# Linear attention and ELU MLP in one kernel: state update fused on VectorE, one kd on ScalarE, an earlier second product, and a split first slice

## The chip, the cores and the metric

The kernel runs on one core of one Trainium2 chip. The metric is the device time of one execution in microseconds (us); lower is better. Six executions fell into a slower state: granted TensorE clocks of 0.856 to 0.992 (0.998 to 1.0 in the fast ones), times of 216.61 to 238.4 us. They are named where they occur, and only fast runs are compared. The profile covers a span some 2 us shorter than the device time of its run: 213.9 us of 215.73 for the kernel before.

## The reference

Two operations follow each other. A decaying linear attention runs over 4 batches, 8 heads, 768 positions and 64 elements per head; its output, as 3072 rows of 512, goes through a two-layer MLP with ELU and 2048 hidden columns.

```python
for b in range(nb):                                   # blocks of positions
    intra = (qb @ kb.T * Dmask) @ vb                  # einsums shortened here
    inter = (qb * lam_pow) @ kv_state
    out[block] = intra + inter
    kv_state = lam_block * kv_state + (kb * rev_pow).T @ vb
h = x @ w_in
g = where(h > 0, h, exp(min(h, 0)) - 1)
return g @ w_out
```

The line that the change is about is the one that updates `kv_state`: an old state times a decay of its head, plus an update.

## The kernel before

The kernel works in chunks `g` of 128 rows of one batch, 24 in all, gathered into tiles of 4, 2, 4, 4, 4, 4 and 2 chunks. One tile passes through 16 slices of 128 hidden columns: the first product `psH`, `e = exp(psH)` and `r = relu(psH)` on ScalarE, `g = min(e - 1, r)` on VectorE, the second product `psM`. The attention of later tiles is put between these. The state of a pair of chunks is updated in two instructions, decay on GpSimd and add on VectorE:

```python
def att_tmp(g, eng="p"):                    # GpSimd: tmp = old state * decay
    ...
    for hh in range(2):
        r = slice(hh * 64, (hh + 1) * 64)
        e.tensor_tensor(
            out=tmp[r], in0=old[r, :, :, r],
            in1=up_p[r].unsqueeze(1).unsqueeze(3).broadcast_to([64, 2, HP, 64]),
            op=ALU.mult,
        )
def att_st(g):                              # VectorE: new state = tmp + psU
    ...
                nc.vector.tensor_tensor(
                    out=new[r, :, :, r], in0=tmps[g][r], in1=pu[r], op=ALU.add
                )
```

From chunk 8 on, q and k are transposed by DMAs that SyncE issues, one for q and one for k of a pair of chunks:

```python
def att_xT(g):
    for j, ts in enumerate((qn, kn)):
        ...
        nc.sync.dma_start_transpose(
            out=dst[:], in_=heads(ts, g, 2).rearrange("p h d -> p (h d)")
        )
```

The loads of later q, k and v are issued by GpSimd. Each is held back by a copy of one element of some g, so that it is not issued before the MLP has come to that point.

```python
def paced_load(s, items):
    ...
        src = gt[t][0:1, n - w, 0:1] if n else gt[t - 1][0:1, NF - 1, 0:1]
        nc.gpsimd.tensor_copy(pace[:], src)
    run_loads(items)

for s, a, b in [(('B', 2), 27, 28), ((1, 2), 28, 29), ((1, 10), 29, 30), ...]:
    at(s, paced_load, s, LOADS[a:b])
```

`(1, 10)` is slice 10 of the second tile, and the element is one of g of the slices just before it, 8 and 9. The load that it paces is that of chunks 12 and 13.

Of the kernel before, what the change touches and what calls it, by code (L numbers as in the profile page):

```python
# [11 lines left out]
ALU = mybir.AluOpType  # L12
# [3 lines left out]
def kernel(  # L16
# [10 lines left out]
    nc = tc.nc  # L27
# [56 lines left out]
    WO = [4, 4, 4, 4]  # L84
# [28 lines left out]
    LOADS = [(0, 1, 'q'), (0, 1, 'k'), (1, 1, 'q'), (1, 1, 'k'), (2, 1, 'q'), (2, 1, 'k'), (3, 1, 'q'), (3, 1, 'k'), (0, 1, 'v'), (1, 1, 'v'), (2, 1, 'v'), (3, 1, 'v'), ('wi', 0), ('wi', 1), ('wi', 2), ('wi', 3), ('kd', 0), ('wi', 4), ('wi', 5), ('kd', 2), ('wi', 6), ('wo', 0), ('wo', 1), (4, 2), ('wo', 2), ('wo', 3), (6, 2), (8, 2), (10, 2), (12, 2), (14, 2), (16, 2), (18, 2), (20, 2), (22, 2)]  # L113

    def run_loads(items):
        for it in items:
            if it[0] == "wi":
                emit_wi(it[1])
            elif it[0] == "wo":
                emit_wo(it[1])  # L120
            elif it[0] == "kd":
                att_kd(it[1], 2, "p")
            else:
                emit_load(*it)

    nc.gpsimd.iota(rel_i[:], pattern=[[1, 128]], base=0, channel_multiplier=-1)
    run_loads(LOADS[:16])

# [173 lines left out]
    def att_S(g, tag="S"):  # L302
        s = ps.tile([128, 2, HP, 128], FP32, tag=tag, bufs=2, name=f"psS{g}")
        for hp in range(HP):
            for hh in range(2):
                r = slice(hh * 64, (hh + 1) * 64)
                nc.tensor.matmul(  # L307
                    s[:, hh, hp, :], lhsT=kT[g][r, hp, :], rhs=qT[g][r, hp, :],
                    start=True, stop=True,
                )  # L310
        pS[g] = s

    def att_mask(g, parts=1):
        P = asb.tile([128, 2, HP, 128], FP16, tag="P", name=f"P{g}", bufs=3)
        s = pS.pop(g)
        w = HP // parts
        for i in range(parts):
            c = slice(i * w, (i + 1) * w)
            nc.vector.tensor_tensor(  # L319
                out=P[:, :, c], in0=s[:, :, c],  # L320
                in1=(mask if g < B else mask1)[:, :, c], op=ALU.mult,
            )
        Pt[g] = P

    def att_O(g, n, tag="S"):
        c = g // B
        po = ps.tile([128, n, HP, 128], FP32, tag=tag, bufs=2, name=f"psO{g}")
        for i in range(n):
            P = Pt.pop(g + i)
            for hp in range(HP):  # L330
                for hh in range(2):
                    r = slice(hh * 64, (hh + 1) * 64)
                    nc.tensor.matmul(  # L333
                        po[r, i, hp, :], lhsT=v_of(g + i, 2 * hp + hh), rhs=P[:, hh, hp, :],
                        start=True, stop=(c == 0), skip_group_check=True,
                    )
                if c == 0:
                    continue
                for hh in range(2):
                    r = slice(hh * 64, (hh + 1) * 64)  # L340
                    nc.tensor.matmul(  # L341
                        po[r, i, hp, :],
                        lhsT=st[(g + i) % B // 2][c % 2][:, (g + i) % 2, hp, r],
                        rhs=qT[g + i][:, hp, :],
                        start=False, stop=True, skip_group_check=True,
                    )
        pS["O", g] = po

    def att_X(g, n, parts=1):
        t, i = where[g]  # L350
        if i == 0:
            xt[t] = asb.tile([128, HP, TS[t] * L], FP16, tag="xt", name=f"xt{t}")
        po = pS.pop(("O", g))
        w = HP // parts
        for j in range(parts):
            c = slice(j * w, (j + 1) * w)
            dst = xt[t][:, c, i * L : (i + n) * L].rearrange("p h (n l) -> p n h l", n=n)
            if g < B:
                copy = nc.vector.tensor_copy if g in () else nc.scalar.copy
                copy(out=dst, in_=po[:, :, c])  # L360
                continue
            nc.vector.tensor_tensor(  # L362
                out=dst, in0=po[:, :, c],
                in1=qs[:, c].unsqueeze(1).broadcast_to([128, n, w, 128]),
                op=ALU.mult,
            )
# [20 lines left out]
    def att_tmp(g, eng="p"):  # L387
        c, b = divmod(g, B)
        if c >= NC - 1 or c == 0:
            return  # L390
        old = st[b // 2][c % 2]
        tmp = asb.tile([128, 2, HP, 64], FP32, tag="tmp", name=f"tmp{g}", bufs=3)
        e = nc.vector if eng == "v" else nc.gpsimd
# [7 lines that stand above are left out]
        tmps[g] = tmp  # L401

    def att_st(g):
        c, b = divmod(g, B)
        if c == NC - 1:
            return
        pu = pS.pop(("U", g))
        new = st[b // 2][(c + 1) % 2]
        for hh in range(2):
            r = slice(hh * 64, (hh + 1) * 64)  # L410
            if c == 0:
                copy = nc.scalar.copy if g in () else nc.vector.tensor_copy
                copy(out=new[r, :, :, r], in_=pu[r])
            else:
                nc.vector.tensor_tensor(  # L415
                    out=new[r, :, :, r], in0=tmps[g][r], in1=pu[r], op=ALU.add
                )
        tmps.pop(g, None)
# [113 lines left out]
    def warm(k, tag="M"):  # L532
        if k <= 0:
            return
        pw = ps.tile([128, 4, 128], FP32, tag=tag, bufs=2, name=f"psW{len(warms)}")
        warms.append(pw)
        for _ in range(k):
            nc.tensor.matmul(
                pw[:, 0:2], lhsT=ident16[:], rhs=any16[:, 0:2], start=True, stop=True
            )  # L540
# [20 lines left out]
    W = [10, 4, 3, 1, 2, 1, 2, 1, 3, 2, 2, 3]  # L561
# [34 lines left out]
    warm(W[8])  # L596
    att_O(0, 1, "M")
    att_X(0, 1)
    att_S(3)
    att_mask(3, 2)  # L600
    late_qs(1, 2)
    warm(W[9])
    att_O(1, 1, "M")
    att_X(1, 1)
    late_qs(2, 3)
    warm(W[10])
    att_O(2, 1, "M")
    att_X(2, 1)
    late_qs(3, 4)
    warm(W[11])  # L610
    att_OX2(3, "H")

    run_loads(LOADS[16:27])
# [8 lines left out]
    XT = {8: ('B', 13), 10: (1, 12), 12: (2, 4), 14: (2, 12), 16: (3, 4), 18: (3, 12), 20: (4, 4), 22: (4, 12)}  # L622

    def visit(g, s0, s1, s2):
        if g in XT:
            at(XT[g], att_xT, g)
        else:
            at(s0, att_T, g, 2, "q")
            at(s0, att_T, g, 2, "k")
            at(s0, att_Te, g, 2, "q", "a")  # L630
            at(s0, att_Te, g, 2, "k", "v" if g in () else "a")
        if g not in ():
            at(s0, att_kd, g, 2, "p" if g in () else "a" if g in () else "v")
        at(s1, att_S, g)
        at(s1, att_S, g + 1)
        at(s1, att_mask, g)
        at(s1, att_mask, g + 1)
        if g in ():
            at(s1, att_kd, g, 2, "p" if g in () else "a" if g in () else "v")
        at(s2, att_O, g, 2)  # L640
        at(s2, att_U, g)
        at(s2, att_X, g, 2)
        at(s2, att_st, g)
        at(s2, att_tmp, g + B)

    for g, vs in [(4, (('B', 1), ('B', 4), ('B', 7))), (6, (('B', 12), (1, 0), (1, 4))), (8, ((1, 6), (1, 10), (1, 14))), (10, ((2, 0), (2, 2), (2, 5))), (12, ((2, 8), (2, 10), (2, 13))), (14, ((3, 0), (3, 2), (3, 5))), (16, ((3, 8), (3, 10), (3, 13))), (18, ((4, 0), (4, 2), (4, 5))), (20, ((4, 8), (4, 10), (4, 13))), (22, ((5, 0), (5, 2), (5, 5)))]:
        visit(g, *vs)
# [9 lines left out]
    for s, a, b in [(('B', 2), 27, 28), ((1, 2), 28, 29), ((1, 10), 29, 30), ((2, 3), 30, 31), ((2, 11), 31, 32), ((3, 3), 32, 33), ((3, 11), 33, 34), ((4, 3), 34, 35)]:  # L657
        at(s, paced_load, s, LOADS[a:b])

    steps = [(('A', 0), (0, 0), []), (('A', 1), (0, 1), []), (('A', 2), (0, 2), []), (('A', 3), (0, 3), []), (('A', 4), (0, 4), []), (('A', 5), (0, 5), []), (('A', 6), (0, 6), []), (('A', 7), (0, 7), []), (('A', 8), (0, 8), []), (('A', 9), (0, 9), []), (('A', 10), (0, 10), []), (('A', 11), (0, 11), []), (('A', 12), (0, 12), [(0, 0, 0), (0, 1, 0)]), (('A', 13), (0, 13), [(0, 0, 1), (0, 1, 1)]), (('A', 14), (0, 14), [(0, 0, 2), (0, 1, 2)]), (('A', 15), (0, 15), [(0, 0, 3), (0, 1, 3)]), (('B', 0), None, [(0, 2, 0), (0, 2, 1), (0, 2, 2), (0, 2, 3)]), (('B', 1), None, [(0, 3, 0), (0, 3, 1), (0, 3, 2), (0, 3, 3)]), (('B', 2), None, [(0, 0, 4), (0, 1, 4), (0, 2, 4), (0, 3, 4)]), (('B', 3), None, [(0, 0, 5), (0, 1, 5), (0, 2, 5), (0, 3, 5)]), (('B', 4), None, [(0, 0, 6), (0, 1, 6), (0, 2, 6), (0, 3, 6)]), (('B', 5), None, [(0, 0, 7), (0, 1, 7), (0, 2, 7), (0, 3, 7)]), (('B', 6), None, [(0, 0, 8), (0, 1, 8), (0, 2, 8), (0, 3, 8)]), (('B', 7), None, [(0, 0, 9), (0, 1, 9), (0, 2, 9), (0, 3, 9)]), (('B', 8), None, [(0, 0, 10), (0, 1, 10), (0, 2, 10), (0, 3, 10)]), (('B', 9), None, [(0, 0, 11), (0, 1, 11), (0, 2, 11), (0, 3, 11)]), (('B', 10), None, [(0, 0, 12), (0, 1, 12), (0, 0, 13), (0, 1, 13)]), (('B', 11), None, [(0, 0, 14), (0, 1, 14), (0, 0, 15), (0, 1, 15)]), (('B', 12), None, [(0, 2, 12), (0, 3, 12), (0, 2, 13), (0, 3, 13)]), (('B', 13), None, [(0, 2, 14), (0, 3, 14), (0, 2, 15), (0, 3, 15)]), ((1, 0), (1, 0), []), ((1, 2), (1, 2), []), ((1, 4), (1, 4), []), ((1, 6), (1, 6), [(1, 0, 0), (1, 1, 0), (1, 0, 1), (1, 1, 1)]), ((1, 8), (1, 8), [(1, 0, 2), (1, 1, 2), (1, 0, 3), (1, 1, 3)]), ((1, 10), (1, 10), [(1, 0, 4), (1, 1, 4), (1, 0, 5), (1, 1, 5)]), ((1, 12), (1, 12), [(1, 0, 6), (1, 1, 6), (1, 0, 7), (1, 1, 7)]), ((1, 14), (1, 14), [(1, 0, 8), (1, 1, 8), (1, 0, 9), (1, 1, 9)]), ((2, 0), (2, 0), [(1, 0, 10), (1, 0, 11)]), ((2, 1), (2, 1), [(1, 0, 12), (1, 0, 13)]), ((2, 2), (2, 2), [(1, 0, 14), (1, 0, 15), (1, 1, 10)]), ((2, 3), (2, 3), [(1, 1, 11), (1, 1, 12)]), ((2, 4), (2, 4), [(1, 1, 13), (1, 1, 14)]), ((2, 5), (2, 5), [(1, 1, 15), (2, 0, 0), (2, 0, 1)]), ((2, 6), (2, 6), [(2, 0, 2), (2, 0, 3)]), ((2, 7), (2, 7), [(2, 0, 4)]), ((2, 8), (2, 8), [(2, 0, 5), (2, 1, 0)]), ((2, 9), (2, 9), [(2, 0, 6), (2, 1, 1)]), ((2, 10), (2, 10), [(2, 0, 7), (2, 1, 2)]), ((2, 11), (2, 11), [(2, 0, 8), (2, 1, 3)]), ((2, 12), (2, 12), [(2, 0, 9), (2, 1, 4)]), ((2, 13), (2, 13), [(2, 0, 10), (2, 1, 5)]), ((2, 14), (2, 14), [(2, 0, 11), (2, 1, 6)]), ((2, 15), (2, 15), [(2, 0, 12), (2, 1, 7)]), ((3, 0), (3, 0), [(2, 0, 13), (2, 1, 8), (2, 0, 14), (2, 1, 9)]), ((3, 1), (3, 1), [(2, 0, 15), (2, 1, 10), (2, 1, 11), (2, 1, 12)]), ((3, 2), (3, 2), [(2, 1, 13), (2, 1, 14), (2, 1, 15), (2, 2, 0)]), ((3, 3), (3, 3), [(2, 2, 1), (2, 2, 2), (2, 2, 3), (2, 2, 4), (2, 2, 5)]), ((3, 4), (3, 4), [(2, 2, 6), (2, 2, 7), (2, 2, 8), (2, 2, 9)]), ((3, 5), (3, 5), [(2, 2, 10), (2, 2, 11), (2, 2, 12), (2, 2, 13)]), ((3, 6), (3, 6), [(2, 2, 14), (2, 2, 15), (2, 3, 0), (2, 3, 1), (2, 3, 2)]), ((3, 7), (3, 7), [(2, 3, 3), (2, 3, 4), (2, 3, 5), (2, 3, 6)]), ((3, 8), (3, 8), [(2, 3, 7), (2, 3, 8), (2, 3, 9), (2, 3, 10)]), ((3, 9), (3, 9), [(2, 3, 11), (2, 3, 12), (2, 3, 13), (2, 3, 14), (2, 3, 15)]), ((3, 10), (3, 10), [(3, 0, 0), (3, 0, 1), (3, 0, 2), (3, 0, 3)]), ((3, 11), (3, 11), [(3, 0, 4), (3, 0, 5), (3, 1, 0), (3, 0, 6)]), ((3, 12), (3, 12), [(3, 1, 1), (3, 0, 7), (3, 1, 2), (3, 0, 8), (3, 1, 3)]), ((3, 13), (3, 13), [(3, 0, 9), (3, 1, 4), (3, 0, 10), (3, 1, 5)]), ((3, 14), (3, 14), [(3, 0, 11), (3, 1, 6)]), ((3, 15), (3, 15), [(3, 0, 12), (3, 1, 7)]), ((4, 0), (4, 0), [(3, 0, 13), (3, 1, 8), (3, 0, 14), (3, 1, 9)]), ((4, 1), (4, 1), [(3, 0, 15), (3, 1, 10), (3, 1, 11), (3, 1, 12)]), ((4, 2), (4, 2), [(3, 1, 13), (3, 1, 14), (3, 1, 15), (3, 2, 0)]), ((4, 3), (4, 3), [(3, 2, 1), (3, 2, 2), (3, 2, 3), (3, 2, 4), (3, 2, 5)]), ((4, 4), (4, 4), [(3, 2, 6), (3, 2, 7), (3, 2, 8), (3, 2, 9)]), ((4, 5), (4, 5), [(3, 2, 10), (3, 2, 11), (3, 2, 12), (3, 2, 13)]), ((4, 6), (4, 6), [(3, 2, 14), (3, 2, 15), (3, 3, 0), (3, 3, 1), (3, 3, 2)]), ((4, 7), (4, 7), [(3, 3, 3), (3, 3, 4), (3, 3, 5), (3, 3, 6)]), ((4, 8), (4, 8), [(3, 3, 7), (3, 3, 8), (3, 3, 9), (3, 3, 10)]), ((4, 9), (4, 9), [(3, 3, 11), (3, 3, 12), (3, 3, 13), (3, 3, 14), (3, 3, 15)]), ((4, 10), (4, 10), [(4, 0, 0), (4, 0, 1), (4, 0, 2), (4, 0, 3)]), ((4, 11), (4, 11), [(4, 0, 4), (4, 0, 5), (4, 1, 0), (4, 0, 6)]), ((4, 12), (4, 12), [(4, 1, 1), (4, 0, 7), (4, 1, 2), (4, 0, 8), (4, 1, 3)]), ((4, 13), (4, 13), [(4, 0, 9), (4, 1, 4), (4, 0, 10), (4, 1, 5)]), ((4, 14), (4, 14), [(4, 0, 11), (4, 1, 6)]), ((4, 15), (4, 15), [(4, 0, 12), (4, 1, 7)]), ((5, 0), (5, 0), [(4, 0, 13), (4, 1, 8), (4, 0, 14), (4, 1, 9)]), ((5, 1), (5, 1), [(4, 0, 15), (4, 1, 10), (4, 1, 11), (4, 1, 12)]), ((5, 2), (5, 2), [(4, 1, 13), (4, 1, 14), (4, 1, 15), (4, 2, 0)]), ((5, 3), (5, 3), [(4, 2, 1), (4, 2, 2), (4, 2, 3), (4, 2, 4), (4, 2, 5)]), ((5, 4), (5, 4), [(4, 2, 6), (4, 2, 7), (4, 2, 8), (4, 2, 9)]), ((5, 5), (5, 5), [(4, 2, 10), (4, 2, 11), (4, 2, 12), (4, 2, 13)]), ((5, 6), (5, 6), [(4, 2, 14), (4, 2, 15), (4, 3, 0), (4, 3, 1), (4, 3, 2)]), ((5, 7), (5, 7), [(4, 3, 3), (4, 3, 4), (4, 3, 5), (4, 3, 6)]), ((5, 8), (5, 8), [(4, 3, 7), (4, 3, 8), (4, 3, 9), (4, 3, 10)]), ((5, 9), (5, 9), [(4, 3, 11), (4, 3, 12), (4, 3, 13), (4, 3, 14), (4, 3, 15)]), ((5, 10), (5, 10), [(5, 0, 0), (5, 0, 1), (5, 0, 2), (5, 0, 3)]), ((5, 11), (5, 11), [(5, 0, 4), (5, 0, 5), (5, 1, 0), (5, 0, 6)]), ((5, 12), (5, 12), [(5, 1, 1), (5, 0, 7), (5, 1, 2), (5, 0, 8), (5, 1, 3)]), ((5, 13), (5, 13), [(5, 0, 9), (5, 1, 4), (5, 0, 10), (5, 1, 5)]), ((5, 14), (5, 14), [(5, 0, 11), (5, 1, 6)]), ((5, 15), (5, 15), [(5, 0, 12), (5, 1, 7)]), ((6, 0), (6, 0), [(5, 0, 13), (5, 1, 8), (5, 0, 14), (5, 1, 9), (5, 0, 15)]), ((6, 2), (6, 2), [(5, 1, 10), (5, 1, 11), (5, 1, 12), (5, 1, 13), (5, 1, 14)]), ((6, 4), (6, 4), [(5, 1, 15), (5, 2, 0), (5, 2, 1), (5, 2, 2), (5, 2, 3), (5, 2, 4)]), ((6, 6), (6, 6), [(5, 2, 5), (5, 2, 6), (5, 2, 7), (5, 2, 8), (5, 2, 9)]), ((6, 8), (6, 8), [(5, 2, 10), (5, 2, 11), (5, 2, 12), (5, 2, 13), (5, 2, 14)]), ((6, 10), (6, 10), [(5, 2, 15), (5, 3, 0), (5, 3, 1), (5, 3, 2), (5, 3, 3), (5, 3, 4)]), ((6, 12), (6, 12), [(5, 3, 5), (5, 3, 6), (5, 3, 7), (5, 3, 8), (5, 3, 9)]), ((6, 14), (6, 14), [(5, 3, 10), (5, 3, 11), (5, 3, 12), (5, 3, 13), (5, 3, 14), (5, 3, 15)]), (('E', 0), None, [(6, 0, 0), (6, 0, 1), (6, 0, 2), (6, 0, 3), (6, 0, 4), (6, 0, 5), (6, 0, 6), (6, 0, 7), (6, 0, 8), (6, 0, 9), (6, 0, 10), (6, 0, 11), (6, 0, 12), (6, 0, 13), (6, 0, 14), (6, 0, 15), (6, 1, 0), (6, 1, 1), (6, 1, 2), (6, 1, 3), (6, 1, 4), (6, 1, 5), (6, 1, 6), (6, 1, 7), (6, 1, 8), (6, 1, 9), (6, 1, 10), (6, 1, 11), (6, 1, 12), (6, 1, 13), (6, 1, 14), (6, 1, 15)])]  # L660
    for s, m1, m2 in steps:
        er = None
        if m1 is not None:
            t, n = m1
            er = mm1(t, n, alt=t == 0 and n in (2, 4, 6))
        do(s)
        if er:
            elu(t, n, *er)
        for t2, i2, n2 in m2:
            mm2(t2, i2, n2, "H" if t2 == 0 and m1 is None and i2 > 1 else "M")  # L670
# [31 lines left out]
```

## Time and profile before

| | before |
|---|---|
| runs (three, before the prediction) | 215.88 to 216.18 us, median 215.9 |
| span of the profiled run | 213.9 us |
| TensorE in the stretch 53 to 97 us | 41.83 of 44.00 us busy |
| VectorE in the same stretch | 43.51 of 44.00 us busy |

The prediction below shows the busy lines, the waits and the timelines. Four more lines of the page belong to them: the shares of the chain that ended last, and the groups of g, of the decay and of the add. In a group's line the count follows the x; after the first bar stand the busy time in us and the mean length in ns, after the second the idle time before it.

```profile
PE 68%; DVE 17%; POOL 5%; issue 3%; DMA 3%; ACT 2%; DVEq 0%; POOLq 0%
...
L478 DVE SCALAR_TENSOR_TENSOR g<-e,r 128x512 f16<-128x512 f32 x93 | 71.1, 781 | 37.6 <-ACT r L465 37.2
...
L396 POOL TENSOR_TENSOR tmp<-st,up_p 64x512 f32<-64x512 f16 x16 | 21.4, 1334 | 5.6 <-DVE st L415 4.9
...
L415 DVE TENSOR_TENSOR st<-tmp,psU 64x512 f16<-64x512 f32 x16 | 10.9, 681 | 0.2
```

VectorE holds 17% of the chain, 36.2 us, and all of it lies in the stretch 53 to 97 us; the mean g of 781 ns mixes those of 0.69 us with those that are stretched beside GpSimd (two in 2.97 us at 61.15). DMAs hold 3%, nearly all of it a load of W_in at 12.7 us. Lines from the timelines: start, length, instruction, and in brackets what ended the idle time before it.

```profile
64.02 1.57 SPq L276 DMA_TRANSPOSE kT<-kn  x1
...
64.25 0.18 POOL L654 COPY pace<-g 1x1 f16<-1x1 f16 x1 [0.68 <-DVE g L478]
64.82 1.21 POOL L72 DMA_DIRECT2D qn<-in_q_dram  x1 [0.39 <-issue]
```

The transpose of k of chunks 10 and 11 is issued at 64.02, the load of chunks 12 and 13 at 64.82. The transpose lands 3.6 us after its issue, at 67.63, and TensorE comes for it at 72.46. There are 0.8 us between the two issues, and the load is released by a g.

### The profile page before, as it was taken

How to read it: one execution, taken by the hardware profiler on the slowest of the kernel's cores; microseconds unless marked ns; L12 is line 12 of the kernel's file. 1: busy time of each engine (PE TensorE's matmuls, PEld its weight loads, DVE VectorE, ACT ScalarE, POOL GpSimd, SP SyncE). 2: the span in 40 equal slices, each digit the busy share in tenths (PEclk: the TensorE clock that was granted, in tenths of full speed). 3: DMA queues.
4: the chain of work that ended last, by engine and by line, in shares of the span. 5: the costliest groups of instructions: out<-in, count | busy, mean ns of one | idle time of the engine just before them, and what ended most of it. 6: DMA issues, size and time to landing. Idle time of an engine off the chain costs nothing.

```text
span 213.9 us, 4112 instructions
## 1 busy us (share of the span) xinstructions
PE 203.0 (95%) x1650; PEld 106.5 (50%) x1650; DVE 150.8 (71%) x193; ACT 126.0 (59%) x238; POOL 83.1 (39%) x85
## 2 busy tenths in 40 slices
PE   5888979999997999989999999999999999999994
PEld 3553425456864454534544544544544544466643
DVE  6774997855999999999698688676557634353321
ACT  6987877306652758664646556655666466676520
POOL 8999957951486447191640610600000000011000
PEclk9999999999999999999999999999999999999999
DMA  5999999999799969999399791499601111011112
GB/s 37 145 153 187 187 198 168 194 156 213 194 136 157 101 149 133 164 73 126 77 152 127 148 135 55 92 153 135 115 0 52 49 49 49 3 51 49 49 52 100
DMA packets 100740, 24.40 MB, mean 114 GB/s; under 512 B 93040, under 2 KB 97904, under 8 KB 100720
## 3 DMA queue, kind: packets, MB, share of 16 engines
q0 software_dynamic: 80368, 14.16, 83.9%
q1 hardware_dynamic: 20208, 9.90, 20.9%
q8 instruction: 13, 0.21, 0.4%
q10 hardware_dynamic: 144, 0.07, 0.1%
q14 instruction: 7, 0.06, 0.1%
HBM read 27.27 MB, written 6.29 MB: 157 GB/s over the span
## 4 chain that ended last, share of the span: by engine, by line
PE 68%; DVE 17%; POOL 5%; issue 3%; DMA 3%; ACT 2%; DVEq 0%; POOLq 0%
PE psM L510 32%; PE psH L432 25%; DVE g L478 8%; DVE P L319 4%; PE psH L450 4%; DMA wi<-in_moe_w_in_dram 3%; DVE st L415 2%; DVE xt L362 2%; POOL qn L72 2%; PE psS L307 2%; POOL kn L72 2%; PE psM L490 2%; POOL vn L72 2%; PE psO L333 2%; PE psO L341 1%
## 5 line engine op out<-in xcount | busy, mean ns | idle before, releaser
L478 DVE SCALAR_TENSOR_TENSOR g<-e,r 128x512 f16<-128x512 f32 x93 | 71.1, 781 | 37.6 <-ACT r L465 37.2
L461 ACT ACTIVATE e<-psH 128x512 f32<-128x512 f32 x96 | 57.4, 597 | 64.2 <-PE psH L432 50.8
L510 PE MATMUL psM<-wo,g 128*128 128x512 f16 x368 | 93.7, 380 | 0.8 <-DVE g L478 0.8
L432 PE MATMUL psH<-xt,wi 128*128 128x512 f16 x320 | 81.3, 379 | 2.4 <-ACT r L465 1.2
L465 ACT ACTIVATE r<-psH 128x512 f16<-128x512 f32 x93 | 55.0, 592 | 0.0
L510 PEld LDWEIGHTS <-g 128*128 128x128 f16 x368 | 34.2, 98 | 39.2 <-DVE g L478 2.3
L432 PEld LDWEIGHTS <-wi 128*128 128x128 f16 x320 | 30.9, 98 | 41.0 <-issue 2.6
L319 DVE TENSOR_TENSOR P<-psS,mask 128x1024 f16<-128x1024 f32 (+1 forms) x28 | 28.7, 1066 | 3.6 <-PE psS L307 3.5
L396 POOL TENSOR_TENSOR tmp<-st,up_p 64x512 f32<-64x512 f16 x16 | 21.4, 1334 | 5.6 <-DVE st L415 4.9
L527 POOL DMA_DIRECT2D out_dram<-osb x2 | 1.1, 574 | 56.0 <-ACT osb L526 51.9
L654 POOL COPY pace<-g 1x1 f16<-1x1 f16 x7 | 2.8, 398 | 45.0 <-DVE g L478 45.0
L362 DVE TENSOR_TENSOR xt<-psO,qs 128x1024 f16<-128x1024 f32 x10 | 12.2, 1221 | 6.7 <-PE psO L341 6.7
L72 POOL DMA_DIRECT2D qn<-in_q_dram x14 | 15.8, 1127 | 2.6 <-issue 2.0
L450 PE MATMUL psH<-xt,wi 128*128 128x256 f16 x128 | 16.5, 273 | 0.0
L72 POOL DMA_DIRECT2D vn<-in_v_dram x14 | 15.2, 1105 | 1.7 <-DMA wo<-in_moe_w_out_dram 1.7
L72 POOL DMA_DIRECT2D kn<-in_k_dram x14 | 15.2, 1087 | 1.4 <-DMA wo<-in_moe_w_out_dram 1.4
L526 ACT COPY osb<-psM 128x512 f32<-128x512 f32 x12 | 7.1, 591 | 13.1 <-PE psM L510 13.0
L450 PEld LDWEIGHTS <-wi 128*128 128x128 f16 x128 | 12.3, 98 | 4.2
L333 PE MATMUL psO<-P,vn 128*64 128x128 f16 x184 | 11.7, 222 | 1.1 <-DVE P L319 0.9
L333 PEld LDWEIGHTS <-vn 128*64 128x64 f16 x184 | 9.8, 109 | 5.7 <-issue 4.8
L294 DVE TENSOR_TENSOR kd<-kn,ks 128x1024 f16<-128x1024 f16 x8 | 11.4, 1427 | 0.0
L415 DVE TENSOR_TENSOR st<-tmp,psU 64x512 f16<-64x512 f32 x16 | 10.9, 681 | 0.2
(58 smaller groups left out, 122.8 us busy)
## 6 DMA issues: line engine op xcount, KB each, us to landing
out_dram<-osb SPq DMA_DIRECT2D x21, 256.0 KB, 2.6
qn<-in_q_dram POOLq DMA_DIRECT2D x10, 256.0 KB, 6.5
kn<-in_k_dram POOLq DMA_DIRECT2D x10, 256.0 KB, 8.3
vn<-in_v_dram POOLq DMA_DIRECT2D x10, 256.0 KB, 8.4
wo<-in_moe_w_out_dram POOLq DMA_DIRECT2D x4, 512.0 KB, 12.8
wi<-in_moe_w_in_dram POOLq DMA_DIRECT2D x2, 512.0 KB, 7.5
wi<-in_moe_w_in_dram POOLq DMA_DIRECT2D x3, 256.0 KB, 5.7
qn<-in_q_dram POOLq DMA_DIRECT2D x4, 128.0 KB, 4.6
```

What stands on the lines that cost most here:

```text
L72: nc.gpsimd.dma_start(out=dst, in_=src[b : b + n, :, rows].rearrange("b h p d -> p (b h) d"))
L319: nc.vector.tensor_tensor(out=P[:, :, c], in0=s[:, :, c], in1=(mask if g < B else mask1)[:, :, c], op=ALU.mult,)
L333: nc.tensor.matmul(po[r, i, hp, :], lhsT=v_of(g + i, 2 * hp + hh), rhs=P[:, hh, hp, :], start=True, stop=(c == 0), skip_group_check=True,)
L362: nc.vector.tensor_tensor(out=dst, in0=po[:, :, c], in1=qs[:, c].unsqueeze(1).broadcast_to([128, n, w, 128]), op=ALU.mult,)
L396: e.tensor_tensor(out=tmp[r], in0=old[r, :, :, r], in1=up_p[r].unsqueeze(1).unsqueeze(3).broadcast_to([64, 2, HP, 64]), op=ALU.mult,)
L415: nc.vector.tensor_tensor(out=new[r, :, :, r], in0=tmps[g][r], in1=pu[r], op=ALU.add)
L432: nc.tensor.matmul(pH[:, lo:hi], lhsT=wi[:, kk, j * 128 : (j + 1) * 128], rhs=xt[t][:, kk, lo:hi], start=(kk == 0), stop=(kk == HP - 1),)
L450: nc.tensor.matmul(pH[:, x * MT : (x + 1) * MT], lhsT=wi[:, kk, j * 128 : (j + 1) * 128], rhs=xt[t][:, kk, :], start=(kk == 0), stop=(kk = ...
L461: nc.scalar.activation(e[:], pH[:], AF.Exp)
L465: nc.scalar.activation(r[:], pH[:], AF.Relu)
L478: nc.vector.scalar_tensor_tensor(out=g, in0=e[:], scalar=-1.0, in1=r[:], op0=ALU.add, op1=ALU.min)
L510: nc.tensor.matmul(pm[:], lhsT=gt[t][:, n, i * L : (i + 1) * L], rhs=wo_t[wo_at[n][0]][:, wo_at[n][1], :], start=(n == 0), stop=(n == NF - 1),
```

## The change

The intent is to take load off VectorE and GpSimd, which stretch each other's instructions between 53 and 97 us: two g take 2.97 us beside decays (at 61.15) and 1.28 without (at 66.42), and a decay takes 1.38 us beside a g (at 62.2) where it took 1.03 with VectorE idle (at 47.7). The decay moves from GpSimd into one fused instruction per head on VectorE, 8 for a pair of chunks, so that GpSimd no longer runs beside VectorE's g. The kd (k times its decay) of one pair of chunks moves to ScalarE, and the second product begins two slices earlier, for which W_out is loaded in other pieces. Slice 0 begins on three chunks before the fourth has its attention.

```diff
-    WO = [4, 4, 4, 4]
+    WO = [2, 2, 4, 4, 4]
-    LOADS = [..., ('wi', 5), ('kd', 2), ('wi', 6), ('wo', 0), ('wo', 1), (4, 2), ('wo', 2), ('wo', 3), ...]
+    LOADS = [..., ('wi', 5), ('kd', 2), ('wo', 0), ('wi', 6), ('wo', 1), ('wo', 2), (4, 2), ('wo', 3), ('wo', 4), ...]
@@ att_tmp
-        if c >= NC - 1 or c == 0:
+        if c >= NC - 1 or c == 0 or 1:
@@ att_st
+            elif 1:
+                old = st[b // 2][c % 2]
+                for hp in range(HP):
+                    nc.vector.scalar_tensor_tensor(
+                        out=new[r, :, hp, r], in0=old[r, :, hp, r],
+                        scalar=up_p[r, hp : hp + 1], in1=pu[r, :, hp, :],
+                        op0=ALU.mult, op1=ALU.add,
+                    )
@@ head: cut, fillers of the clock left out
+    for x, f in zip([('O', 0), ('S', 3), ('qs', 0), ('O', 1), ..., ('O2', 3, 'S'), ('L', 0, 384)], W[8:]):
+        ...
+        elif x[0] == "L":
+            mm1_mm(0, x[1], lo, x[2], ...)      # slice 0, columns of three chunks
+            cut[x[1]] = x[2]
@@ visit
-            at(s0, att_kd, g, 2, "p" if g in () else "a" if g in () else "v")
+            at(s0, att_kd, g, 2, "p" if g in () else "a" if g in (8,) else "v")
@@ steps: slice, then the blocks of the second product behind it (one line, cut)
-  (A,10) [], (A,11) [], (A,12) [(0,0,0),(0,1,0)], (A,13) [(0,0,1),(0,1,1)], ...   # 14 steps of B
+  (A,10) [(0,0,0),(0,1,0)], (A,11) [(0,0,1),(0,1,1)], (A,12) ..., (A,13) ..., ... # 13 steps of B
@@ the first step of chunks 6 and 7 and the transposes of 8 and 9 one step earlier in B, since B has one step fewer
```

The list of pacing points stays the same (its indices into `LOADS` move by one).

## The prediction

The 0.29 can be had from the trace as an estimate: P takes 687 ns for 512 columns and 1218 ns for 1024, and on a straight line through these 128 columns take 0.29 us. The two holds of 0.09 stand for the step between the halves of a state update: the two st at 68.76 are 0.70 us from start to start, where g, as long, follow in 0.60. The mask row is an activation with a scale for each partition.

> **What bounds the kernel now.** First the busy lines of the page, then the waits of TensorE, then the chain that ended last, then the timelines of TensorE, VectorE and GpSimd where the chain leaves TensorE.
>
> ```profile
> PE 203.0 (95%) x1650; PEld 106.5 (50%) x1650; DVE 150.8 (71%) x193; ACT 126.0 (59%) x238; POOL 83.1 (39%) x85
> ...
> PE psH L432 <- ACT r L465: 1.2, 3, 0.7
> PE psO L333 <- DVE P L319: 0.9, 2, 0.5
> PE psM L510 <- DVE g L478: 0.8, 1, 0.8
> ...
> PE psH L432 <- DVE xt L362: 0.5, 1, 0.5
> ```
>
> TensorE is the bound: 203.0 of 213.9 us busy. A 512-column matmul is shown with a length of about 0.38 us, but in the chain four of them take 0.86 us, 0.216 us each. So the tail of the last one hides about 0.16 us of every wait, and a wait is really that much longer than its row says. The wait rows above are three waits for r in stage A (the slices of the first tile, 17 to 36 us), and four waits for P, g and xt in the stretch 53 to 97 us, where VectorE is busy without a gap. From 97 us to the last matmul the timeline of TensorE has no wait at all, and there is nothing to win there. Before 17 us the start is bound by loads.
>
> Stage A in the timeline of TensorE:
>
> ```profile
> 27.59 2.00 PE L432 MATMUL psH<-xt,wi 128*128 128x512 f16 x8 [0.31 <-ACT r L465]
> 29.78 1.02 PE L432 MATMUL psH<-xt,wi 128*128 128x512 f16 x4 [0.19 <-ACT r L465]
> 30.64 0.59 PE L510 MATMUL psM<-wo,g 128*128 128x512 f16 x2
> 31.95 1.02 PE L432 MATMUL psH<-xt,wi 128*128 128x512 f16 x4 [0.72 <-ACT r L465]
> ```
>
> Slices 10 and 11, slice 12, two matmuls of the second product, slice 13. Slice 13 waits for the PSUM bank of slice 11, whose r is late because its e needs the buffer of e of slice 8, and g of slice 8 stood on VectorE behind two state copies. Real losses: 27.59 minus the 27.11 at which the eight matmuls before could have ended is 0.47; 0.12 inside the first row; 0.36 before 29.78; 0.88 before 31.95. Sum 1.8 us.
>
> In the stretch that VectorE bounds, the timelines of GpSimd (one row) and VectorE:
>
> ```profile
> 60.19 3.38 POOL L396 TENSOR_TENSOR tmp<-st,up_p 64x512 f32<-64x512 f16 x2
> ...
> 57.76 1.39 DVE L415 TENSOR_TENSOR st<-tmp,psU 64x512 f16<-64x512 f32 x2
> ...
> 61.15 2.97 DVE L478 SCALAR_TENSOR_TENSOR g<-e,r 128x512 f16<-128x512 f32 x2
> 64.15 2.36 DVE L319 TENSOR_TENSOR P<-psS,mask 128x1024 f16<-128x1024 f32 x2
> 66.42 1.28 DVE L478 SCALAR_TENSOR_TENSOR g<-e,r 128x512 f16<-128x512 f32 x2
> ...
> 71.02 2.06 DVE L294 TENSOR_TENSOR kd<-kn,ks 128x1024 f16<-128x1024 f16 x1
> ```
>
> Two g take 2.97 us while GpSimd runs the state decay (tmp), and 1.28 us when it doesn't. The kd at 71.02, beside the next decay, takes 2.06; others take 1.21. That is what makes P late at 64.15, and with it both attention waits of TensorE.
>
> [...] The mask row of ScalarE (128x128 with such a scale, 8 in 2.5 us, or four in 1.26) measures what I need: about 0.29 us apiece in a row.
>
> **The change, part by part.**
>
> *Fused state update.* Removed: 16 GpSimd decays (21.4 us of an engine that isn't the bound) and 16 VectorE adds. Added: per pair of chunks 8 scalar_tensor_tensor of 64x128, one SBUF tensor, one PSUM tensor, a pointer scalar. [...] as g is 0.69 long and follows in 0.60, I take 0.21 from start to start. 8 x 0.21 plus two holds of 0.09 is 1.85 us, against 1.39: VectorE pays 0.46 more for each of 8 updates, four of them in the bounded stretch (57.8, 68.8, 79.5 and 92.4): +1.8 us. Given back there, from the single rows of the VectorE timeline: six g of 1.52 or 0.96 and one kd, 0.84 each for six of these and 0.28 for one: 5.3 us. The last two of these g end at 97.6.
>
> *kd of 8-9 to ScalarE.* VectorE loses one kd of 1.14 us start to start, at 60.0. ScalarE gets 8 multiplies of 128x128 at 0.29, 2.35 us, between r of slice 6 (ends 58.55) and e of slice 8 (was 59.20, now 60.9). r of slice 8 then ends at about 61.95; TensorE wants that bank for slice 12 at 62.26. It fits by 0.3 us.
>
> VectorE net in the stretch: 5.3 + 1.1 - 1.8 = 4.6 us freed, against TensorE waits of 0.56 + 0.68 + 0.65 + 0.97 + 0.14 = 3.0 us (gaps plus the hidden tail). Placing the rows anew: state done 59.6, g of slice 4 to 60.5, g of slice 6 to 61.1, g of slice 8 not before 62.0 (its r), P 62.6 to 63.75, second P to 64.95. TensorE comes for them at 64.87 and 65.3, so 0.56 and 0.68 go. xt then ends about 67.3 and TensorE is free for it at 67.05: 0.25 of 0.65 remain. The wait at 96.2 goes, as VectorE gains more than a microsecond on TensorE by then. **Saved: 2.75 us.**
>
> *Second product from slice 10.* Twelve instead of eight of its matmuls stand in stage A. Slice 13 still cannot start before 31.95, since the chain g 8, e 11, r 11 is not touched; but before it now stand six of these matmuls instead of two. Slice 10 at 27.59, two to 28.9, slice 11 to 29.76 (its bank was free at 28.52), two to 30.2, slice 12 to 31.05, two to 31.5, wait. Gain: four matmuls moved into waiting time, 4 x 0.216. **Saved: 0.86 us.** All later work up to 53 us follows without a wait and moves up.
>
> *W_out in pieces.* The same bytes in another order. From the arrivals on the queue (wi 5 at 25.1, wi 6 at 27.7, then 2.5 us for each W_out quarter of 1 MB read) I estimate: first half piece at 26.4 (wanted 28.45), wi 6 at 29.0 (wanted 30.2), second half piece at 30.2 (wanted 31.05). No wait; without this part the second product could not start before 30.2. It saves nothing by itself.
>
> *Slice 0 on three chunks.* The wait of 0.46 us before slice 0 at 16.98 ends earlier, but slice 1 starts at 18.18 because its weights land at 18.13, whatever slice 0 does:
>
> ```profile
> 18.18 4.69 PE L432 MATMUL psH<-xt,wi 128*128 128x512 f16 x20 [0.18 <-DMA wi<-in_moe_w_in_dram]
> ```
>
> Its order of loads is not changed. VectorE's first g could start 0.3 us earlier but is held by the kd of GpSimd until 20.4 anyway. **Saved: 0.** The repeated first qs column costs ScalarE 0.3 us, in the same shadow.
>
> Sum: 2.75 + 0.86 + 0 = 3.6 us; 215.9 - 3.6 = 212.3 us, 1.7% faster.
>
> **The rivals.**
>
> 1. *VectorE stays the bound.* The small fused instructions could cost 0.35 instead of 0.21 (a pointer scalar and 64 instructions, none of this form in the trace). Then an update costs 2.9, 1.5 more than before; the attention waits still nearly vanish, but xt is late by the old amount and the wait at 96 us comes back. Saved about 1.1 in all: 214.8. Against it: the 128x128 forms on VectorE without pointer take 0.22 to 0.23 us.
> 2. *ScalarE becomes the wait.* The eight multiplies delay slice 8's g; if they take 0.4 each, slice 12 waits 0.6 and both P are late by as much: about 1 us lost, 213.3. For it: the margin of 0.3. Against it: the mask row.
> 3. *Everything recoverable is recovered.* All waits in stage A (with those at 18 and 19 us, 2.3), in the stretch (3.0) and before slice 0 (0.65) make 6 us: 209.9. Half of the excess over 3.6 would need the wi loads to land earlier or g of slice 8 to be ready earlier; neither is touched.
> 4. *A load takes its place.* TensorE reaching the transposes of chunks 4 and 5 earlier would run into their k, which lands at 36.9; but four more matmuls now stand ahead of them, so they come at the old time.
>
> **Range and chances.** Rival 1 in part or whole, about one in six, stretches the range to 213.8; rival 3 in part to 211.0. Under 2% gain means 211.6 or more, that is less than 4.3 us saved; my sum is 0.7 short of it. Faster 0.22, within 2% 0.77, slower 0.01: nothing here adds TensorE work.
>
> **What would show it.** In the changed profile: GpSimd busy down by about 21 us; g beside chunk work uniformly 0.68 (0.91 right after a state update), none of 1.52 after 50 us; the fused row 64 x about 0.29 long; in the waits of TensorE the P, g rows gone, xt about 0.1 to 0.3, r near 0.7; slice 1 still at about 18.2; start of slice 13 still near 31.95, with six second-product matmuls before it. The prediction is wrong if the fused row takes over 0.35 apiece, if the wi pieces land at other times, or if a new wait on ScalarE stands at 60 to 63 us.

## The result and the profile after

The changed kernel ran at 214.48, 214.62 and 215.07 us, and once at 217.84 (granted clock 0.992); the median of the four is 214.84. The kernel before had 216.03 beside it (four runs, 215.88 to 216.18). The ratio is 0.994, interval 0.9919 to 0.9961: the same within 2%, and 1.3 us gained (0.006 of 216) where 3.6 were predicted. The time lies above the predicted range. Ratios here and below are the mean time of one kernel's fast runs over that of the other's of the same rounds, so not quite the ratio of the medians quoted.

The page of the changed kernel, in the order of the lines shown of before: the busy line, the chain's shares, the groups of g and of the fused update.

```profile
PE 203.5 (96%) x1654; PEld 107.4 (51%) x1654; DVE 148.6 (70%) x240; ACT 128.4 (60%) x247; POOL 61.9 (29%) x70
...
PE 73%; DMA 10%; DVE 7%; POOL 7%; issue 1%; ACT 1%; POOLq 0%; ACTq 0%
...
L487 DVE SCALAR_TENSOR_TENSOR g<-e,r 128x512 f16<-128x512 f32 x93 | 63.6, 699 | 37.4 <-ACT r L474 37.0
...
L418 DVE SCALAR_TENSOR_TENSOR st<-st,up_p,psU 64x128 f16<-64x128 f16 x64 | 18.2, 345 | 0.1
```

GpSimd is busy 21.2 us less, and the mean g fell from 781 to 699 ns: the stretching by the decay is gone. VectorE's share of the chain fell from 17 to 7%. But DMA rose from 3 to 10%, which nothing in the change asks for. The fused instruction is 345 ns long, where the prediction took 290.

The waits of TensorE in the changed kernel (total us, times, longest us); the rows for P and xt of before are gone from it:

```profile
PE psS L308 <- DMA kT<-kn: 0.9, 1, 0.9
PE psH L441 <- DMA wi<-in_moe_w_in_dram: 0.6, 2, 0.4
...
PE psH L441 <- ACT r L474: 0.5, 2, 0.3
PE psM L519 <- DVE osb L533: 0.3, 1, 0.3
```

The first row is new, and it is the longest after the head. The chain that ended last leads through it; here it is between 57 and 72 us in the changed kernel (start, length, what):

```profile
57.27 6.51 DMA kn<-in_k_dram
63.78 0.02 issue
63.80 7.50 DMA kT<-kn
71.30 0.05 issue
71.34 0.62 PE psS L308 x16
```

The transpose of k of chunks 10 and 11 is issued at 63.80, 0.2 us earlier than before, and takes 7.50 us to land in place of 3.6. TensorE could have started psS at 70.28, where its four matmuls from 69.42 are through (4 x 0.216), and starts at 71.34: 1.06 us later. About 0.1 of it stands at this place without a wait too (experiment 1). The GpSimd timeline of the changed kernel shows what went ahead of the transpose:

```profile
62.15 0.18 POOL L665 COPY pace<-g 1x1 f16<-1x1 f16 x1 [2.58 <-DVE g L487]
62.72 1.15 POOL L72 DMA_DIRECT2D qn<-in_q_dram  x1 [0.39 <-issue]
```

The pacing copy waits for g of slices 8 and 9, as before, but that g is ready 2.1 us earlier, because VectorE is. So the load is issued at 62.72 in place of 64.82, and 1.1 us ahead of the transpose in place of 0.8 behind it. The transpose is issued from SyncE and depends on data of its own, so it did not move along. With the load behind it the transpose took 3.6 us, with the load ahead of it 7.50.

The second shortfall is on VectorE. The timeline of the changed kernel, VectorE first and TensorE after it:

```profile
78.37 2.29 DVE L418 SCALAR_TENSOR_TENSOR st<-st,up_p,psU 64x128 f16<-64x128 f16 x8
...
81.41 0.69 DVE L533 COPY osb<-psM 128x512 f32<-128x512 f32 x1
...
81.44 0.39 PE L519 MATMUL psM<-wo,g 128*128 128x512 f16 x1
82.15 0.38 PE L519 MATMUL psM<-wo,g 128*128 128x512 f16 x1 [0.33 <-DVE osb L533]
```

A state update is 8 instructions in 2.29 us, 0.286 from start to start; predicted were 1.85 and 0.21, and the add of before took 1.39. Behind it a g and then the copy `osb` that frees a bank for TensorE are late. TensorE loses 0.17 and 0.50 us here, and 0.17 and 0.16 waiting for g near 95 us: 1.0 us, where 1.11 was lost to g at 96 us before and no loss was predicted.

Stage A of the changed kernel, in the timeline of TensorE: slice 10 at 28.08, slice 13 at 32.27.

```profile
28.08 1.02 PE L441 MATMUL psH<-xt,wi 128*128 128x512 f16 x4 [0.31 <-ACT r L474]
28.94 0.59 PE L519 MATMUL psM<-wo,g 128*128 128x512 f16 x2
...
31.53 0.59 PE L519 MATMUL psM<-wo,g 128*128 128x512 f16 x2
32.27 1.02 PE L441 MATMUL psH<-xt,wi 128*128 128x512 f16 x4 [0.15 <-ACT r L474]
```

From slice 10 to 13 it is 4.19 us, 4.36 before, with six matmuls of the second product in it instead of two. That part came in as predicted: 0.86 for the four moved, 0.17 from the distance. Slice 10 itself starts 0.49 us later than before (28.08 against 27.59), since the third piece of W_in landed at 19.68 in place of 19.19. That landing lies between 18.7 and 20.7 us over all profiled runs, and between 19.1 and 20.7 in the four that keep the old order of W_in and W_out. So it is taken as scatter of the head and not as the change.

| term | predicted | measured in this profile |
|---|---|---|
| waits for P | +1.24 | +1.24 |
| wait for xt | +0.40 | +0.38 |
| wait at 96 us | +1.11 | +0.1 (1.11 less 1.0 of new waits behind updates) |
| new wait for kT | none | -1.06 |
| second product from slice 10 | +0.86 | +1.03 |
| head | 0 | -0.49 (taken as scatter) |
| sum | 3.6 | 1.2 |

The terms of waits are from start to start: the gap of the row and the hidden tail of about 0.165 us. The span fell from 213.9 to 212.7, which agrees with the sum.

### The profile page after: what moved, and what is told of

The parts are those of the page before. It is cut to its first block, busy times and chain, and to the rows that moved or that the text cites. A ratio compares the mean times of both kernels' runs of the same rounds, so it can differ in the third digit from the quotient of the medians.

```text
span 212.7 us, 4157 instructions
## 1 busy us (share of the span) xinstructions
PE 203.5 (96%) x1654; PEld 107.4 (51%) x1654; DVE 148.6 (70%) x240; ACT 128.4 (60%) x247; POOL 61.9 (29%) x70
## 4 chain that ended last, share of the span: by engine, by line
PE 73%; DMA 10%; DVE 7%; POOL 7%; issue 1%; ACT 1%; POOLq 0%; ACTq 0%
PE psM L519 35%; PE psH L441 26%; PE psH L459 4%; DMA kT<-kn 4%; DMA kn<-in_k_dram 3%; DMA wi<-in_moe_w_in_dram 3%; PE psS L308 2%; POOL qn L72 2%; PE psO L334 2%; DVE g L487 2%; PE psO L342 2%; POOL kn L72 2%; PE psM L499 2%; POOL vn L72 2%; DVE st L414 1%
## 5 line engine op out<-in xcount | busy, mean ns | idle before, releaser
L487 DVE SCALAR_TENSOR_TENSOR g<-e,r 128x512 f16<-128x512 f32 x93 | 63.6, 699 | 37.4 <-ACT r L474 37.0
L441 PE MATMUL psH<-xt,wi 128*128 128x512 f16 (+2 forms) x324 | 81.5, 376 | 1.2 <-DMA wi<-in_moe_w_in_dram 0.6
L418 DVE SCALAR_TENSOR_TENSOR st<-st,up_p,psU 64x128 f16<-64x128 f16 x64 | 18.2, 345 | 0.1
L72 POOL DMA_DIRECT2D qn<-in_q_dram x14 | 15.3, 1095 | 4.6 <-DMA qn<-in_q_dram 1.9
L342 PE MATMUL psO<-qT,st 128*64 128x128 f16 x160 | 10.0, 219 | 0.0
L547 PE MATMUL psW<-ident 128*128 128x256 f16 x34 | 8.0, 360 | 1.7 <-DVE ident L140 1.7
```

The costliest lines, as they stand in the source:

```text
L72: nc.gpsimd.dma_start(out=dst, in_=src[b : b + n, :, rows].rearrange("b h p d -> p (b h) d"))
L342: nc.tensor.matmul(po[r, i, hp, :], lhsT=st[(g + i) % B // 2][c % 2][:, (g + i) % 2, hp, r], rhs=qT[g + i][:, hp, :], start=False, stop=Tr ...
L418: nc.vector.scalar_tensor_tensor(out=new[r, :, hp, r], in0=old[r, :, hp, r], scalar=up_p[r, hp : hp + 1], in1=pu[r, :, hp, :], op0=ALU.mul ...
L441: nc.tensor.matmul(pH[:, lo:hi], lhsT=wi[:, kk, j * 128 : (j + 1) * 128], rhs=xt[t][:, kk, lo:hi], start=(kk == 0), stop=(kk == HP - 1),)
L487: nc.vector.scalar_tensor_tensor(out=g, in0=e[:], scalar=-1.0, in1=r[:], op0=ALU.add, op1=ALU.min)
```

## The experiments

Two theories. **The load**: the load of chunks 12 and 13, released early by the faster g, goes ahead of the transpose of chunks 10 and 11 and makes it land late (7.50 us after its issue in place of 3.6); that costs 1 us or more. **The pointer**: the fused instruction is longer than estimated (345 ns in place of 290) since its scalar is a pointer to one value per partition, and what it costs VectorE keeps about 1 us of waits in place. Rivals: the bank that `osb` frees is late for another reason, the fusion itself gives nothing, or the gain of stage A is not real. Times are medians of all runs, slow ones included; the ratio is that of fast runs alone to the before kernel of the same rounds. There were three batches, each on a chip of its own: experiments 1 to 4 (median before 215.82), 5 to 7 (215.90), 8 and 9 (216.12). Where ratios of different batches are set beside each other below, the change of chip is a further uncertainty.

**1. Load paced two slices later** (an edit of the changed kernel):

```diff
-  ((1, 10), 30, 31)
+  ((1, 12), 30, 31)
```

> The changed kernel, but the load of chunks 12-13 waits for g of slice 10 of the second tile instead of slice 8, so it is issued near 65 us, about where the kernel before issued it (64.8), and not at 62.7. Theory (the transpose of k of chunks 10-11 is slow because that load went ahead of it in the DMA engines): the transpose issued near 63.8 lands in about 3.6 us as before, not in 7.5; the wait of psS for kT (0.9 us, really 1.06) goes; about 1.0 us faster than the changed kernel, near 213.8. Rival (the transpose is slow for another reason, or the wait only moves to the next visit): the transpose still takes over 6 us or the psS wait shows up later, time within 0.3 us of 214.7.

Measured: 213.20 us, ratio 0.988 (0.986 to 0.990), against 0.994 for the change. The issues of the transpose and of the load, and the matmuls that use it, in the timelines of this run:

```profile
64.74 1.24 SPq L277 DMA_TRANSPOSE kT<-kn  x1
...
66.22 1.15 POOL L72 DMA_DIRECT2D qn<-in_q_dram  x1
...
70.91 0.62 PE L308 MATMUL psS<-qT,kT 64*128 64x128 f16 x16
```

The load now follows the transpose by 1.5 us, the transpose takes 4.75 us, and psS starts 0.96 us after the four matmuls of the slice before it, of which these need 0.86: there is no wait. The whole edit is one index. It gains 0.006 of 216, 1.3 us, and the intervals of the two ratios don't touch: the theory of the load holds. The profiled run lost 0.84 us to a late piece of W_out at 34.95 (taken up in the last experiment).

**2. One `osb` on ScalarE:**

```diff
-            if i % 2:
+            if i % 2 and (t, i) != (1, 1):
```

> The changed kernel, but the output copy of chunk 1 of the second tile is done by ScalarE and not by VectorE, where it stands behind eight fused updates and a g. Theory (the wait of psM at 82.15 is the price of the longer update on VectorE, 2.29 us against 1.39): the psM waits of 0.17 and 0.50 us near 82 go, 0.5 to 0.7 us faster than the changed kernel, near 214.1. Rival (TensorE is short of g there anyhow): the psM wait for the copy goes but one for g takes its place, and less than 0.2 us is won.

Measured: 215.09 us, ratio 0.9922 (0.9887 to 0.9957), six runs from 213.04 to 218.83, two of them slow. Alone it is not conclusive. Its profile fell in the slow state (clock 0.992); it shows only that the osb row is gone and the row for kT is there.

**3. An immediate in place of the pointer scalar** (wrong result, to measure the operand):

```diff
-                        scalar=up_p[r, hp : hp + 1], in1=pu[r, :, hp, :],
+                        scalar=0.5, in1=pu[r, :, hp, :],
```

> The changed kernel with an immediate 0.5 in place of the per-partition decay in the 64 fused updates: a wrong result on purpose. Theory (the pointer scalar makes each of them 345 ns long and 0.286 us from start to start, where I had taken 0.29 long and 0.21 apart): they fall to about 0.29 long and 0.21 apart, eight take 1.7 to 1.85 us. Rival (it is the fixed cost of a small instruction with one PSUM input): they stay within 0.02 us of 345 ns and eight take 2.3 us. Time: 0.3 to 0.6 us faster than the changed kernel under the theory, equal under the rival.

Measured: 214.85 us (four runs, one slow), ratio 0.9926 (0.990 to 0.9952). The group of the fused instruction in this run:

```profile
L418 DVE SCALAR_TENSOR_TENSOR st<-st,psU 64x128 f16<-64x128 f16 x64 | 14.2, 281 | 0.1
```

281 ns against 345: the pointer scalar costs 64 ns per instruction, and eight of them take 1.79 us against 2.29. That is just the length that the prediction took for the form with a pointer (0.29 and 1.85). But the time hardly moved, where 0.3 to 0.6 us were expected: the wait for kT grew from 0.9 to 1.9 us in the profile. TensorE comes for it 6.1 us after its issue in place of 6.5, and the transpose, issued behind the load again, takes 8.1 us. The two shortfalls stand in series, and the second is only seen when the first is removed.

**4. The change without the fusion** (decay on GpSimd and add on VectorE as before):

```diff
-        if c >= NC - 1 or c == 0 or 1:
+        if c >= NC - 1 or c == 0:
-            elif 1:
+            elif 0:
```

> The changed kernel with the old state update back (decay on GpSimd, add on VectorE), all else kept. It tells what the fusion by itself is worth. If fusing is worth what I predicted in the stretch that VectorE bounds (part of 2.75 us, say 1.5 to 2), this is 1.5 us or so slower than the changed kernel, near 216.2. If its price (longer updates, loads issued earlier) eats its gain, it is within 0.5 us of 214.7, the transposes of chunks 10-11 land in 4 us again, and g next to a decay are 1.52 us long again.

Measured: 214.51 us, ratio 0.9937 (0.9916 to 0.9959), the same as with it. g is up to 1.52 us long again, as expected, but the transpose did not land in 4 us: the load is issued first here too (63.77 and 64.16), and the transpose takes 6.3 us. It lands at 70.46, before TensorE comes at 71.3, so there is no wait. Taken alone the ratio says that the fusion is worth nothing. Beside experiment 1, in the same rounds (0.988), and beside experiment 8 it says so only while the load stands in its way.

**5. The fusion alone** on the kernel before, nothing else of the change:

```diff
-        if c >= NC - 1 or c == 0:
+        if c >= NC - 1 or c == 0 or 1:
+            elif 1:
+                ... (att_st as in the change)
```

> The kernel before with the fused state update and nothing else of the change. The fused update is measured at 2.29 us a pair against 1.39, so VectorE gains 5.3 - 4 x 0.9 = 1.7 us in the stretch of 53 to 97 us. Theory: the gain on the waits of TensorE for P, xt and g (3.0 us before) is 1 to 2 us, and the load of chunks 12-13, no longer held by the decay on GpSimd, goes out before 64 us and makes the transpose of k of chunks 10-11 land after 69 us instead of 67.6; if that comes in time for S of chunk 10 (72.5) it costs nothing: time 214.2 to 215. Rival (the load's early issue costs in any case): a psS wait for kT of about 1 us stands at 72, time 215.5 to 216.

Measured: 214.67 us, ratio 0.9949 (0.9933 to 0.9965), 1.1 us gained. In its profile the load is issued before the transpose too (64.25 and 64.73) and the transpose takes 6.9 us. It lands at 71.6, and TensorE, which isn't as far here, comes at 71.8: 0.2 us of margin. So in this run the early load costs nothing yet.

**6. kd of chunks 8 and 9 alone** on ScalarE, on the kernel before:

```diff
-            at(s0, att_kd, g, 2, "p" if g in () else "a" if g in () else "v")
+            at(s0, att_kd, g, 2, "p" if g in () else "a" if g in (8,) else "v")
```

> The kernel before with kd of chunks 8-9 on ScalarE and nothing else. From the run with the old state update, whose waits in the stretch were 2.0 us in place of 3.0: about 1.0 us faster than before, near 214.9. Rival (ScalarE's 2.35 us delay r of slice 8 and give it back): within 0.3 us of before.

Measured: 214.95 us, ratio 0.997 (0.9939 to 1.0001). Five runs lie within 214.78 to 215.06; the one that was profiled took 217.21 and shows a W_in wait of 1.9 us at the head, so its profile doesn't stand for the others. Yet it shows that this part alone moves the load ahead of the transpose as well (65.22 and 65.62): the transpose took 8.4 us and TensorE waited 1.1 us for it. So the wait does not need the fusion; whether the other five runs have it was not seen.

**7. The second product and W_out alone**, on the kernel before:

```diff
-    WO = [4, 4, 4, 4]
+    WO = [2, 2, 4, 4, 4]
... (LOADS and steps as in the change)
```

> The kernel before with the second product from slice 10 and W_out in pieces 2,2,4,4,4, nothing else. Predicted: 0.86 us faster, near 215.0. Rival, from two of four runs, in which TensorE waited about 1.0 us at 35 us for the W_out piece of blocks 4 to 7 (landing 34.9 and 35.1 instead of 32.7): the piece comes too late as often as not and nothing is left on the mean, 215.5 to 216.

Measured: 215.19 us, ratio 0.9967 (0.9951 to 0.9984), 0.7 us gained. The 0.86 of the prediction lies within the interval (0.3 to 1.1). **Slice 0 on three chunks alone**, on the kernel before:

```diff
+    for x, f in zip([('O', 0), ('S', 3), ..., ('L', 0, 384)], W[8:]):
+        ... (head and steps loop as in the change, with its W)
```

> The kernel before with slice 0 begun on three chunks (and the new order of the head) and nothing else. Predicted: nothing, since slice 1 waits for its weights at 18.1 whatever slice 0 does; within 0.3 us of before. Rival: the head jitters with the arrival of these weights, and an earlier slice 0 gains up to 0.4 us in runs where they land early.

Measured: 216.24 us, ratio 1.0012 (0.9996 to 1.0028): nothing, as predicted.

**8. Pacing together with the other edits**, each on the changed kernel. First with the osb of experiment 2:

```diff
-            if i % 2:
+            if i % 2 and (t, i) != (1, 1):
-  ((1, 10), 30, 31)
+  ((1, 12), 30, 31)
```

> The changed kernel with both: the load of chunks 12-13 paced one step later and the output copy of chunk 1 of the second tile on ScalarE. Theory: 1.6 us (as measured for the pacing alone) and another 0.5 for the psM wait at 82: near 212.7, ratio to before about 0.986. Rival (ScalarE's copy delays e and TensorE waits there instead, or g is the next to be late): no better than 213.2.

Measured: 213.01 us, ratio 0.9853 (0.983 to 0.9876), five fast runs from 212.88 to 213.17; the profiled one was slow (238.4, clock 0.856) and is not read. The intervals of this and of pacing alone (0.986 to 0.990) overlap, so the 0.6 us that the osb seems to add is not shown. With pacing and the immediate of experiment 3 (`scalar=0.5`, wrong result again):

> The changed kernel with the later pacing and an immediate in place of the pointer scalar (wrong result on purpose). With the immediate alone eight updates took 1.79 us in place of 2.29, but the time did not move, as the transpose wait grew to 2.0 us in the run profiled. Theory: with that wait out of the way the 0.5 us per update count: the waits of psM near 82 (0.67) and 94 (0.33) shrink to under 0.4 together, and the time is 0.5 to 0.7 us below the 213.2 of the pacing alone. Rival (the updates are off the path): 213.0 to 213.3.

Measured: 212.39 us, ratio 0.9823 (0.9798 to 0.9848), a larger gain over the pacing alone (1.2 us by ratios of two batches) than the 0.5 to 0.7 expected. With pacing and the old state update (`or 1` taken out, `elif 0`, as in experiment 4):

> The changed kernel with the later pacing but the old state update. It tells what the fusion is worth once no load stands in the way. Theory: the waits for P, xt and g stay at about 2.0 us in the stretch (0.27, 0.64, 0.95, 0.14) against 0.27 + 0.67 + 0.33 = 1.3 with fusion, so the fusion is worth 0.7 us: near 213.9 against 213.2. Rival (the fusion was only good for freeing GpSimd): equal to 213.2.

Measured: 215.16 us, ratio 0.9966 (0.9937 to 0.9996). Beside pacing with the fusion (0.988, another batch) the fusion is worth 0.0086 of 216, 1.9 us, once the load is out of its way. Within one batch, the paced change against experiment 4 (0.988 and 0.9937, neither with a kT wait in its profile), it is 1.2 us. Without the fusion pacing gains nothing (0.9966 after 0.9937). The stretch 53 to 97 us in the windows of the kernel before, of the change and of the run with pacing and immediate (TensorE, its weight loads, VectorE, ScalarE and GpSimd busy in us with counts, granted clock, DMA share, GB/s):

```profile
53.00:97.00 44.00, 41.83 (x435) 23.67 (x430) 43.51 (x48) 27.43 (x51) 26.45 (x24) 1.00 1.42 140
```

```profile
53.00:97.00 44.00, 42.66 (x427) 23.47 (x426) 41.81 (x73) 29.37 (x59) 15.44 (x16) 1.00 1.54 148
```

```profile
53.00:97.00 44.00, 43.88 (x447) 24.38 (x446) 40.99 (x75) 31.12 (x62) 15.77 (x16) 1.00 1.57 151
```

TensorE is busy 41.83, then 42.66, then 43.88 of 44: with both causes removed no wait over 0.3 us is left there, and the time is that of the prediction.

**9. Pacing and osb with W_out in six pieces**, against the W_out wait seen in experiment 1:

```diff
-    WO = [2, 2, 4, 4, 4]
+    WO = [2, 2, 2, 2, 4, 4]
... (LOADS: one piece more ahead of the load of chunks 4 and 5; pacing and osb as in 8)
```

> The changed kernel with later pacing, the output copy on ScalarE and W_out in pieces 2,2,2,2,4,4, so that blocks 4 and 5, wanted at 34.4, land 1.25 us before blocks 6 and 7. Theory (the W_out wait of about 1.0 us at 35 us, seen in two of the profiled runs, is only for blocks 4 and 5): it goes in the runs that have it, 0.3 to 0.5 us better on the mean than without the split: near 212.3. Rival (another piece costs as much in issue and order as it gives): no better than the version with pieces 2,2,4,4,4.

Measured: 213.35 us, ratio 0.9866 (0.9843 to 0.989). The W_out wait is not in its profile, but the time is not better than pacing with osb (0.9853). So the theory that this wait is common missed; how often it occurs in runs that were not profiled stays open.

The best correct version is thus pacing with osb, 213.01 us. It beats the kernel before by 1.5% and the change by 0.9% (0.9853 over 0.994), but pacing alone (0.988) is not told apart from it.

## Why the prediction was wrong

What the runs showed about the order of the two transfers, in all profiled runs that were fast (us from the start of the span for the issues, us from issue to landing for the last column):

| run | load of 12 and 13 | transpose of k, 10 and 11 | landing after |
|---|---|---|---|
| transpose first: before | 64.82 | 64.02 | 3.6 |
| second product alone | 64.11 | 63.76 | 3.4 |
| slice 0 alone | 65.12 | 64.35 | 3.6 |
| pacing | 66.22 | 64.74 | 4.75 |
| pacing, immediate | 65.22 | 63.89 | 4.8 |
| pacing, old update | 66.08 | 63.69 | 3.1 |
| pacing, osb, six pieces | 65.62 | 63.80 | 3.3 |
| load first: the change | 62.72 | 63.80 | 7.5 |
| immediate | 63.45 | 64.90 | 8.1 |
| no fusion | 63.77 | 64.16 | 6.3 |
| fusion alone | 64.25 | 64.73 | 6.9 |
| kd alone | 65.22 | 65.62 | 8.4 |

The other pairs of chunks show the same, in every profile, that of the kernel before included. The transposes of k of chunks 16 and 17 and of 20 and 21 are issued 1.5 to 1.8 us behind a load and take 8.9 to 9.8 us in each of the 14 profiles, the two slow ones included (9.6 and 8.9 in the kernel before, 9.8 and 9.5 in the change); those of 12, 18 and 22, with the next load behind them or none, take 3.1 to 3.4. In the kernel before, the transpose of 16 and 17 and the load of a later pair (timelines of SyncE, then of GpSimd):

```profile
105.42 2.14 SPq L276 DMA_TRANSPOSE kT<-kn  x1
...
103.62 1.21 POOL L72 DMA_DIRECT2D qn<-in_q_dram  x1 [0.39 <-issue]
```

This one takes 9.63 us and costs nothing, since it lands at 115.05 and TensorE comes at 115.97. So the price of a load issued first could have been read before the prediction. Order is not all that sets the time: the pairs 8 and 14, with no load issued within 2 us of them, took 3.1 to 6.3 us.

Point by point:

- **TensorE bounds, waits of 3.0 us in the stretch are to be won, and nothing before 17 or after 97 us:** right. No wait stands after 97 us in the change either.
- **Contention of GpSimd and VectorE goes:** right. GpSimd fell by 21.2 us (predicted about 21), no g of 1.52 us is left after 50 us, and the waits for P are gone. The wait for xt left 0.27 of 0.65 (predicted 0.25). Which instructions are stretched, the trace before shows only in part. P and xt never ran beside a decay in the stretch; st did and was not stretched (0.69 us at 69.46, 0.64 of it beside one). The kd at 71.02 took 2.06 us beside a decay, but the kd at 60.01 ran 1.04 us beside one and still took 1.21: there the decay was the longer one, 1.93 us.
- **Second product from slice 10, 0.86 us:** right, 1.03 in the profile and 0.7 in the run alone. Slice 13 started at 32.27, not 31.95; the whole of stage A had moved by the scatter of the head.
- **W_out in pieces, no wait:** right in the profile of the change; in two others (pacing, and immediate) a piece was late by 0.8 to 0.9 us.
- **Slice 0, nothing:** right. Slice 1 started at 18.30 (18.18 before).
- **ScalarE as the wait (rival 2):** did not come. The eight multiplies took 2.44 us (2.35 predicted); VectorE waits 0.50 us for r at 61.3, TensorE not at all.
- **A load takes its place (rival 4):** looked for at the wrong load. The prediction had the rival for chunks 4 and 5. It said "A load takes its place", but asked only whether TensorE would run into a load that lands at a fixed time. It did not ask which issues VectorE's progress releases. A g that is 2.1 us earlier released a load 2.1 us earlier, and this load delayed a transpose with a wait of 1.06 us. **This is the step that failed**, by about 1 us in the profiled run. Pacing it back gave 1.3 us.
- **The fused update, "about 0.29 long", "0.21 from start to start" and "1.85 us":** mis-sized. It measured 345 ns, 0.286 and 2.29 us. With an immediate it is 281 ns and 1.79 us, so the estimate fits the form without a pointer and the whole difference is the pointer. Four updates in the stretch cost 0.44 more each, 1.8 us of VectorE. So of the 1.11 us in "the wait at 96.2 goes" only 0.1 came in: 0.33 stayed near 95 us, and 0.67 came new near 82. With the load paced and an immediate, 0.18 of this 1.0 is left, and the time fell by 1.2 us (0.988 to 0.9823).
- **Rival 1 (VectorE stays the bound, 214.8)** named the right time, but by luck. Its 0.35 us was meant from start to start, where 0.286 was measured (that 345 ns is the length is chance). Loss on VectorE came back, as it said; but xt was not late by the old amount, and the other half of the shortfall was the load. It had been given one chance in six on the strength of 128x128 forms without a pointer (0.22 to 0.23 us), which are not the form in question.

The two causes make 1.3 + 1.2 = 2.5 us by ratios (0.994 to 0.988 to 0.9823, from three sets of rounds, each ratio good to about 0.5 us), the gap between 212.3 predicted and 214.8 measured. With both removed the run gave 212.39 us. So the sum of the prediction agrees, within this, with a kernel in which the load stays behind the transpose and the scalar costs nothing. That the sums agree to 0.1 us is chance: the head scattered by 0.5 us in the profile alone.

What stays open: why the landing of the third piece of W_in, and in some runs of a piece of W_out, scatters. That the load's issue ahead of the transpose makes it late is shown by the pacing (4.75 us to landing in place of 7.50); whether and how the two take DMA engines from each other is not, since it is inferred from order and duration and no run here took the trace of single packets apart.

## What to carry to other kernels

When an engine becomes faster, list every DMA whose issue it releases, and check each against the transfers that another queue has in flight or is about to issue: an earlier load can be worse than a late one (here 2.1 us earlier, and TensorE lost 1.06). Test parts of a change also together and with the suspected obstacle removed, since the same fusion was worth 0 us behind the load and 1.2 to 1.9 us without it. And take an instruction's cost from its own operands: a short form that is issued 64 times has its price in what it costs apiece (345 ns with the pointer, 281 with an immediate).
